# A fused attention and two-layer-MLP kernel: one weight loaded a step earlier, evictions placed ahead of conversion passes, and a lasting buffer for queries and keys

## The chip, the cores and the metric

The kernel runs on one core of a Trainium2 chip. The metric is the device time of one execution in microseconds (us); the number quoted for a kernel is the median of its runs. Before the change it is 1781.75 us (three runs, 1778.74 to 1783.21).

## The reference

Eight sequences of 576 tokens go through three stages. `q`, `k` and `v` have 8 heads of 64 columns; the model width is 512, the hidden width 2048.

```python
# 1: attention inside chunks of 64 tokens, head by head
scores = scale * np.matmul(q_c, k_c.transpose(0, 1, 2, 4, 3))
attn = softmax(scores)                      # last axis, max subtracted
x = heads_side_by_side(np.matmul(attn, v_c))
# 2: layer norm and a two-matmul block with its residual
xn = (x - mu) / np.sqrt(var + 1e-06) * g_ln
x = x + np.maximum(xn @ w_ch1, 0.0) @ w_ch2
# 3: a rank-32 mix over the tokens, then a second block
u = x + (x.transpose(0, 2, 1) @ U @ V).transpose(0, 2, 1)
out = u + np.maximum(u @ w2_ch1, 0.0) @ w2_ch2
```

The weights `U`, `V` and the four matrices arrive as 64-bit floats and are turned into 32-bit ones on the chip, by a handful of bit operations on each tile.

## The kernel before, in words

The 4608 tokens are 36 tiles of 128. Stage 1 and 2 work on 12 groups j = 0 to 11 of three tiles, stage 3 on 9 groups j = 12 to 20 of four. A group meets 16 slices f of the hidden width. One pair (j, f) is one **step** g of the main loop (lines 841 to 864): `g1` (line 638) issues twelve matmuls into the tile `psh`, then ScalarE writes the high part of the ReLU (line 648) and VectorE the low part (line 649); then the loop issues whatever `plan[g]` holds; then `g2` (line 650) multiplies the step two back into the accumulators `acc`, and after f = 15 `finish` (line 665) has VectorE add the accumulators to the residual (line 668), which frees their PSUM banks. Every product is made of three float32r matmuls (high by high, high by low, low by high). The first matmul of the next group into an accumulator waits for that eviction.

Groups 0 and 1 alternate in steps 2 to 31; from step 32 a group has 16 steps in a row. Steps 0 to 27 also convert the first set of weights; a PSUM bank for `psh` is single up to step 31 and doubled later.

All else is hung into the steps by `at(g, fn, ...)`, by hand (`manual_schedule`): each engine runs its instructions in the order in which the program issues them, and a DMA is issued by an engine too. SyncE issues the loads of `q`, `k`, `v` and the stores; ScalarE issues the second set of weights (`load_w`, line 113) and the round trips through DRAM that transpose a tile (`spread` and `gather`, lines 539 and 545). So a DMA that has to wait on ScalarE holds the ReLU behind it.

What the change touches:

- `load_ut` (line 201), in step 27: four SyncE loads of `U` into a raw tile, then its conversion (`conv_act` on ScalarE, `conv_bits` and `conv_hi` on VectorE, lines 81 to 105, and lines 211 and 212). The conversion's scratch takes the buffer `q6` or `k6` in turn.
- `load_qk` (line 253): queries and keys of group j, as 32-partition pieces in 128-byte runs. A group of 6 chunks that lies in one sequence is 32 DMAs, one that crosses two sequences 64 (`chunk_runs` yields two runs; groups 4, 7 and 10). Each group takes a new tile in the one buffer `q6` and the one buffer `k6`, so that its first DMA waits until the last tile of the group before has been read. Lines 740 to 743 cut the DMAs into parts, one for a step: 4 parts from the 12th step after g = 16(n-1) for n = 2, 4 from the 8th for n = 3, 9 from the 4th for n = 4, else 9 from the 3rd, where n + 1 is the group loaded.
- `st_A` (line 308): two VectorE transposes (lines 311 and 312) read one tile's share of the two buffers. The scores' matmuls into `psm` (`st_Bd`) need them, in the next step or the one after.
- `pre_a`, `pre_b` and `pre_c` (lines 165 to 182): conversion of the second set of weights, one weight tile every three and a half steps from step 58 on: `pre_a` two ScalarE and two VectorE passes, `pre_b` three VectorE passes, `pre_c` a store issued by ScalarE. They stand in `plan[g]`, so ahead of `g2` and `finish` of the same step.

Of the kernel before, what the change touches and what calls it, by code (L numbers as in the profile page):

```python
# [18 lines left out]
def fused_kernel(ctx, tc, q, k, v, g_ln, w1_a, w2_a, U, V, w1_b, w2_b, out):  # L19
    nc = tc.nc  # L20
# [86 lines left out]
    def raw_tile():  # L107
        return rawp.tile([P, DM, 2], I32, tag="raw", name="raw")
# [89 lines left out]
    def conv_f32(raw, rows, n, out):  # L198
        return conv_hi(conv_bits(conv_act(raw, rows, n)), out)

    def load_ut():
        Ui = U.bitcast(I32)
        raw = raw_tile()
        v = raw.rearrange("p (t r) w -> p t (r w)", r=RK)
        nc.sync.dma_start(out=v[:, 0:4], in_=Ui[0:512].rearrange("(t p) r -> p t r", p=P))
        nc.sync.dma_start(out=v[0:64, 4], in_=Ui[512:576])
        nc.sync.dma_start(out=v[64:128, 4], in_=Ui[0:64])
        nc.sync.dma_start(out=v[:, 5:9], in_=Ui[64:576].rearrange("(t p) r -> p t r", p=P))
        o = ut[:, 0:9].rearrange("p t r -> p (t r)")
        a, c = conv_f32(raw, P, 9 * RK, o)  # L210
        nc.vector.tensor_tensor(out=c, in0=c, in1=a, op=ALU.mult)
        nc.vector.tensor_tensor(out=o, in0=o, in1=c, op=ALU.add)

        nc.gpsimd.memset(ut[0:64, 9], 0.0)
        nc.gpsimd.tensor_copy(out=ut[64:128, 9], in_=ut[64:128, 4])
        nc.gpsimd.memset(ut[64:128, 4], 0.0)
# [36 lines left out]
    def load_qk(j, part, parts_):  # L253
        todo = []
        for nm in ("q6", "k6"):
            if part == 0:
                qk[nm, j] = qkp.tile([P, 4, 4 * TPB, 32], F32, tag=nm, name=nm)
        for off, n, b, s0 in chunk_runs(2 * TPB * j, 2 * TPB):
            for nm, src in (("q6", q), ("k6", k)):
                for g in range(4):  # L260
                    for pr in range(4):
                        todo.append((
                            qk[nm, j][32 * g:32 * g + 32, pr, 2 * off:2 * (off + n), :],
                            src[b, 2 * pr + g // 2, s0:s0 + n * CH, (g % 2) * 32:(g % 2) * 32 + 32].rearrange("(a j) i -> j a i", j=32),
                        ))
        for o, i_ in todo[part * len(todo) // parts_:(part + 1) * len(todo) // parts_]:
            nc.sync.dma_start(out=o, in_=i_)  # L267
# [40 lines left out]
    def st_A(i):  # L308
        j, t = divmod(i, TPB)
        qt = t1.tile([P, 4, P], F32, tag="qt", name="qt")  # L310
        nc.vector.transpose(out=qt.rearrange("p h (a j) -> p h a j", a=4), in_=qk["q6", j][:, :, 4 * t:4 * t + 4, :])
        nc.vector.transpose(out=pl["k"][:, 0].rearrange("p h (a j) -> p h a j", a=4), in_=qk["k6", j][:, :, 4 * t:4 * t + 4, :])
        state["qt", i] = qt

    qn = {}
# [362 lines left out]
    with tc.manual_schedule():  # L678
# [14 lines left out]
        for n in range(2, NB + NB2):  # L693
            g = NF * (n - 1)
            ends = []
            for t, i in enumerate(tiles_of(n)):
                s = g + (0, 4, 6, 8)[t]
                if n == 2:
                    s = (10, 15, 24)[t]
                    at(s - 6, load_qk_nat, i)  # L700
                    at(s, st_A_pe, i)
                    at(s + 1, st_B, i)
                    at(s + 2, st_C, i)
                    at(s + 3, st_D, i)
                    at(s + 3, load_v, i + 1)
                    if t == 0:
                        at(5, kv_tiles, i)
                        at(6, load_v, i)
                    ends += [(pos[0, NF - 1] - 1 + t, st_N, i), (pos[0, NF - 1] + t, st_E_pe, i)]
                elif n < NB:  # L710
                    s = g + {3: (2, 5, 8), 4: (-1, 2, 5)}.get(n, (-2, 1, 5))[t]
                    at(s - (1 if n < 5 or t == 0 else 2), st_A, i)
                    at(s, st_Bd, i)
                    at(s + 1, st_Cd, i)
                    at(s + 2, gather, 2 * NT + i)
                    at(s + 3, st_T, i)
                    at(s + 5, st_D, i)
                    if i + 1 < NT:
                        at(s + 5, load_v, i + 1)
                    s += 4 if n == 3 else 6  # L720
                    at(s + (n == 3), st_N, i)
                    at(s + 1, st_S, i)
                    at(s + 2, gather, i)
                    at(s + 3, st_E, i)
                else:
                    at(s + 1, u_load, i)
                    r = i % 9
                    if r in (0, 4):
                        b = 2 * (i // 9) + (r == 4)
                        at(s - 5, z_load, b, 0)  # L730
                        at(s - 4, z_sum, b)
                        at(s - 4, z_load, b, 1)
                        at(s - 2, z_rep, b)
                    at(s + 2, st_U, i)
                    at(s + 4, st_US, i)
                    at(s + 5, gather, NT + i)
                    at(s + 6, st_UE, i)
            for x in sorted(ends, key=lambda x: (x[0], x[1] is st_N)):
                at(*x)
            if 2 <= n < NB - 1:  # L740
                parts_ = 4 if n < 4 else 9
                for part in range(parts_):
                    at(g + {2: 12, 3: 8, 4: 4}.get(n, 3) + part, load_qk, n + 1, part, parts_)
        for n in range(NB + NB2):
            g = pos[n, NF - 1] + 1
            at(g + LAG + 2, store, n)
# [20 lines left out]
        EARLY = (2, 4, 6, 8)  # L767
        for p in range(len(EARLY), NP):
            at(max(p - 4, 2), weight, p)
        at(27, load_ut)  # L770
        at(NF * (NB - 2) + 9, load_V)
        at(NF * (NB - 2) + 13, make_vst)
        PRE_G = 58
# [67 lines left out]
        for g in range(len(seq) + LAG + 3):  # L841
            if g < pos[1, 0] + LAG:
                banks.update(h=("h0", "m0"), m=("m1", "h1", "z"))
            elif g < 10:
                banks.update(h=("h0", "m0"), m=())
            elif g <= pos[0, NF - 1] + LAG:
                banks.update(h=("h0",), m=("m0",))
            elif g == pos[0, NF - 1] + LAG + 1:
                banks.update(h=("h0",), m=("m0", "acc1", "acc2"))
            elif g < 2 * NF:  # L850
                banks.update(h=("h0", "acc0"), m=("m0", "acc1", "acc2"))
            elif g <= 2 * NF + 1:
                banks.update(h=("h0",), m=("m0",))
            else:
                banks.update(h=("h0", "h1"), m=("m0",) if pos[NB, 0] + LAG - 1 <= g <= pos[NB, NF - 1] + LAG else ("m0", "m1"))
            if g < len(seq):
                g1(*seq[g])
            for fn, a in plan.get(g, ()):
                fn(*a)
            if LAG <= g < len(seq) + LAG:  # L860
                j, f = seq[g - LAG]
                g2(j, f)
                if f == NF - 1:
                    finish(j)


_INS = ["q", "k", "v", "moe_g_ln", "moe_w_ch1", "moe_w_ch2", "moe2_U", "moe2_V", "moe2_w_ch1", "moe2_w_ch2"]
# [21 lines left out]
```

## Time and profile before

| what | value |
|---|---|
| median of the runs | 1781.75 us |
| the profiled execution's own time | 1782.99 us |
| its span, first to last instruction | 1781.0 us |
| TensorE busy | 1719.9 us, 97% |
| VectorE, ScalarE, GpSimd busy | 779.1, 372.3, 184.1 us |
| mean granted TensorE clock | 0.988 of full |

The page counts matmuls as PE and weight loads as PEld; `psh` is the output of `g1`, `acc` of `g2`, `psm` of the attention. A timeline row gives the start and length of an instruction (or of several alike, with their count), its engine and line, output and inputs, and in brackets the idle time of the engine just before it and what ended that. A row of waits gives who waited for what, the sum, the number of times and the longest. In a row of windows the busy time of each engine stands with its instruction count, then PEclk, the granted TensorE clock as a share of 2.4 GHz (0.50 is 1.2 GHz), then the DMA engines' share and GB/s. SPq and ACTq are the instruction queues of SyncE and ScalarE; all rows are from the one profiled execution, in us from its start.

### The profile page before, as it was taken

What the parts mean: (1) busy time and instruction counts of PE and PEld (TensorE: products, weight loads), DVE (VectorE), ACT (ScalarE), POOL (GpSimd) and SP (SyncE); (2) the same over time, 40 slices, a digit from 0 to 9 for tenths busy, and PEclk for the clock granted to TensorE, in tenths of its full rate; (3) what the DMA queues carried; (4) which work ended last, traced back from release to release, by engine and by line L of the source; (5) the groups of instructions that cost most, each with busy time, mean ns of one, the idle gap of its engine ahead of it and who ended that gap; (6) DMA issues with size and microseconds to landing.
All of it is one profiled execution on the core that took longest, in us unless ns stands there. A gap on an engine that the chain in (4) does not pass through costs nothing.

```text
span 1781.0 us, 25335 instructions
## 1 busy us (share of the span) xinstructions
PE 1719.9 (97%) x9960; PEld 1458.7 (82%) x9960; DVE 779.1 (44%) x1496; ACT 372.3 (21%) x666; POOL 184.1 (10%) x199
## 2 busy tenths in 40 slices
PE   6799898999999999999999999999999999999999
PEld 5678787888888888888888888888888888888887
DVE  6898744466656666565645312121212121212111
ACT  4333311122122222222223211111111111111110
POOL 1000001011010110101111010101010101000000
PEclk8899999999999999999999999999999999999999
DMA  7343324446465564655436312221212121212100
GB/s 169 95 129 108 80 76 98 107 123 161 108 150 138 129 148 105 166 130 135 120 107 200 96 47 72 53 72 48 71 47 72 48 74 45 66 30 60 30 24 24
DMA packets 293095, 167.48 MB, mean 94 GB/s; under 512 B 189424, under 2 KB 251888, under 8 KB 292976
## 3 DMA queue, kind: packets, MB, share of 16 engines
q1 hardware_dynamic: 212048, 93.48, 20.3%
q10 hardware_dynamic: 80928, 72.39, 15.1%
q8 instruction: 78, 1.28, 0.3%
q14 instruction: 41, 0.34, 0.1%
HBM read 112.82 MB, written 52.95 MB: 93 GB/s over the span
## 4 chain that ended last, share of the span: by engine, by line
PE 83%; DVE 8%; DMA 3%; issue 2%; SPq 2%; ACT 1%; POOL 1%; ACTq 0%; DVEq 0%; POOLq 0%
PE psh L60 40%; PE acc L60 39%; PE psm L60 2%; DMA raw<-in_moe_w_ch 1%; PE zps L60 1%; DVE act L649 1%; DVE cvt L95 1%; DVE cvt L103 1%; SPq L294 1%; ACT act L648 1%; DMA k<-in_k 1%; SPq L267 0%; DVE cvt L104 0%; DVE bs L468 0%; DVE cvt L94 0%
## 5 line engine op out<-in xcount | busy, mean ns | idle before, releaser
L60 PE MATMUL psh<-act,w0h 128*128 128x384 f32 (+1 forms) x2688 | 756.5, 362 | 18.4 <-DVE act L649 13.0
L60 PEld LDWEIGHTS psh<-act,w0h 128*128 128x128 f32 x2688 | 503.2, 190 | 84.8 <-DVE act L649 16.3
L60 PE MATMUL psh<-act,w0l 128*128 128x384 f32 (+1 forms) x1344 | 486.8, 362 | 1.0 <-DVE w0l L147 1.0
L649 DVE SCALAR_TENSOR_TENSOR hk<-psh,hq 128x512 fp32r<-128x512 f32 (+1 forms) x160 | 108.6, 679 | 629.3 <-ACT hq L648 629.3
L60 PE MATMUL acc<-w1h,act 128*128 128x512 f32 x1056 | 366.1, 401 | 4.8 <-DVE x L668 3.9
L60 PEld LDWEIGHTS psh<-act,w0l 128*128 128x128 f32 x1344 | 255.4, 190 | 23.8 <-DVE w0l L147 1.4
L60 PE MATMUL acc<-w1h,hq 128*128 128x512 f32 x624 | 243.0, 389 | 0.0
L60 PE MATMUL acc<-w1l,hq 128*128 128x512 f32 x624 | 243.0, 389 | 0.0
L60 PE MATMUL acc<-w1h,hk 128*128 128x512 f32 x624 | 242.9, 389 | 0.0
L60 PEld LDWEIGHTS acc<-w1h,act 128*128 128x128 f32 x1056 | 198.9, 188 | 51.6 <-ACT act L648 6.8
L648 ACT ACTIVATE hq<-psh 128x512 fp32r<-128x512 f32 (+1 forms) x160 | 94.0, 588 | 647.6 <-PE psh L60 647.6
L60 PE MATMUL acc<-w1l,act 128*128 128x512 f32 x528 | 209.1, 396 | 0.0
L649 DVE SCALAR_TENSOR_TENSOR act<-psh,act 128x384 fp32r<-128x384 f32 x176 | 97.7, 555 | 232.2 <-ACT act L648 231.8
L648 ACT ACTIVATE act<-psh 128x384 fp32r<-128x384 f32 x176 | 86.2, 490 | 440.0 <-PE psh L60 268.5
L555 POOL TENSOR_TENSOR act<-wT,act 128x512 fp32r<-128x512 f32 x63 | 81.2, 1289 | 898.5 <-ACT act L554 888.9
L60 PEld LDWEIGHTS acc<-w1h,hq 128*128 128x128 f32 x624 | 117.1, 188 | 25.6 <-ACT hq L648 1.7
L60 PEld LDWEIGHTS acc<-w1h,hk 128*128 128x128 f32 x624 | 117.1, 188 | 24.4
L60 PEld LDWEIGHTS acc<-w1l,hq 128*128 128x128 f32 x624 | 117.1, 188 | 24.1
L60 PEld LDWEIGHTS acc<-w1l,act 128*128 128x128 f32 x528 | 99.4, 188 | 16.0
L472 POOL TENSOR_SCALAR rs<-mv 128x1 f32<-128x1 f32 x36 | 8.9, 247 | 526.5 <-DVE mv L470 518.3
L554 ACT CAST act<-wT 128x512 fp32r<-128x512 f32 x63 | 39.2, 622 | 99.3 <-DVE wT L552 99.3
L552 DVE STREAM_TRANSPOSE wT<-w 128x512 f32<-128x512 f32 x63 | 44.3, 703 | 7.2 <-DMA wd<-v_pl 2.8
(106 smaller groups left out, 1039.7 us busy)
## 6 DMA issues: line engine op xcount, KB each, us to landing
w<-sp ACTq DMA_DIRECT2D x90, 256.0 KB, 2.7
x1d<-x SPq DMA_DIRECT2D x36, 256.0 KB, 2.6
x<-x1d SPq DMA_DIRECT2D x36, 256.0 KB, 3.4
sp<-x ACTq DMA_DIRECT2D x144, 64.0 KB, 1.8
out<-x SPq DMA_DIRECT2D x36, 256.0 KB, 2.2
v_pl<-in_v SPq DMA_DIRECT2D x132, 64.0 KB, 2.7
raw<-in_moe_w_ch SPq DMA_DIRECT2D x64, 128.0 KB, 2.8
raw<-in_moe_w_ch SPq DMA_DIRECT2D x16, 512.0 KB, 3.7
```

The costliest lines, as they stand in the source:

```text
L60: nc.tensor.matmul(o, lhsT=l, rhs=r, start=start, stop=stop)
L95: nc.vector.scalar_tensor_tensor(out=bi, in0=hw, scalar=-0x40000000, in1=bi, op0=ALU.bitwise_and, op1=ALU.bitwise_or)
L103: nc.vector.scalar_tensor_tensor(out=c, in0=d, scalar=2.0 ** -20, in1=c, op0=ALU.mult, op1=ALU.add)
L294: nc.sync.dma_start(out=pl["vbd"][pp, :, c, 64 * h2:64 * h2 + 64] if E0 <= i < PE_T else pl["v"][pp, i % 2 if i < E0 else 0, :, c, :], in_ ...
L472: nc.gpsimd.tensor_scalar(out=rs, in0=mv[:, 1:2], scalar1=1e-6, scalar2=None, op0=ALU.add)
L552: nc.vector.transpose(out=x.rearrange("p k (a j) -> p a k j", a=4), in_=w.rearrange("p a (k i) -> p a k i", k=KT))
L554: nc.scalar.copy(out=hi, in_=x)
L555: nc.gpsimd.tensor_tensor(out=lo, in0=x, in1=f32(hi), op=ALU.subtract)
L648: nc.scalar.activation(out=hi, in_=ps, func=AF.Relu)
L649: nc.vector.scalar_tensor_tensor(out=lo, in0=ps, scalar=0.0, in1=f32(hi), op0=ALU.max, op1=ALU.subtract)
```

## The change

`U` is loaded in step 27 and converted in step 28. Queries and keys get one tile each in `q6` and `k6` for the whole of stage 1, so a DMA of the next group waits only for the reads of the part that it overwrites. Their DMAs are cut anew: 4 parts from the 13th step for n = 2; else 6 parts for a group in one sequence and 8 (n = 3) or 10 for one that crosses two; from the 5th step for n = 3, from the 4th for one run, from the 0th for two. In the steps in which a group from j = 2 on ends, `pre_a`, `pre_b` and `pre_c` are issued after `finish` instead of before `g2`.

```diff
--- before.py
+++ after.py
@@ -198,14 +198,18 @@
     def conv_f32(raw, rows, n, out):
         return conv_hi(conv_bits(conv_act(raw, rows, n)), out)
 
-    def load_ut():
+    uraw = {}
+
+    def load_U():
         Ui = U.bitcast(I32)
-        raw = raw_tile()
+        raw = uraw[0] = raw_tile()
         v = raw.rearrange("p (t r) w -> p t (r w)", r=RK)
         nc.sync.dma_start(out=v[:, 0:4], in_=Ui[0:512].rearrange("(t p) r -> p t r", p=P))
         nc.sync.dma_start(out=v[0:64, 4], in_=Ui[512:576])
         nc.sync.dma_start(out=v[64:128, 4], in_=Ui[0:64])
         nc.sync.dma_start(out=v[:, 5:9], in_=Ui[64:576].rearrange("(t p) r -> p t r", p=P))
+    def make_ut():
+        raw = uraw.pop(0)
         o = ut[:, 0:9].rearrange("p t r -> p (t r)")
         a, c = conv_f32(raw, P, 9 * RK, o)
         nc.vector.tensor_tensor(out=c, in0=c, in1=a, op=ALU.mult)
@@ -253,14 +257,14 @@
     def load_qk(j, part, parts_):
         todo = []
         for nm in ("q6", "k6"):
-            if part == 0:
-                qk[nm, j] = qkp.tile([P, 4, 4 * TPB, 32], F32, tag=nm, name=nm)
+            if nm not in qk:
+                qk[nm] = qkp.tile([P, 4, 4 * TPB, 32], F32, tag=nm, name=nm)
         for off, n, b, s0 in chunk_runs(2 * TPB * j, 2 * TPB):
             for nm, src in (("q6", q), ("k6", k)):
                 for g in range(4):
                     for pr in range(4):
                         todo.append((
-                            qk[nm, j][32 * g:32 * g + 32, pr, 2 * off:2 * (off + n), :],
+                            qk[nm][32 * g:32 * g + 32, pr, 2 * off:2 * (off + n), :],
                             src[b, 2 * pr + g // 2, s0:s0 + n * CH, (g % 2) * 32:(g % 2) * 32 + 32].rearrange("(a j) i -> j a i", j=32),
                         ))
         for o, i_ in todo[part * len(todo) // parts_:(part + 1) * len(todo) // parts_]:
@@ -308,8 +312,8 @@
     def st_A(i):
         j, t = divmod(i, TPB)
         qt = t1.tile([P, 4, P], F32, tag="qt", name="qt")
-        nc.vector.transpose(out=qt.rearrange("p h (a j) -> p h a j", a=4), in_=qk["q6", j][:, :, 4 * t:4 * t + 4, :])
-        nc.vector.transpose(out=pl["k"][:, 0].rearrange("p h (a j) -> p h a j", a=4), in_=qk["k6", j][:, :, 4 * t:4 * t + 4, :])
+        nc.vector.transpose(out=qt.rearrange("p h (a j) -> p h a j", a=4), in_=qk["q6"][:, :, 4 * t:4 * t + 4, :])
+        nc.vector.transpose(out=pl["k"][:, 0].rearrange("p h (a j) -> p h a j", a=4), in_=qk["k6"][:, :, 4 * t:4 * t + 4, :])
         state["qt", i] = qt
 
     qn = {}
@@ -738,9 +742,10 @@
             for x in sorted(ends, key=lambda x: (x[0], x[1] is st_N)):
                 at(*x)
             if 2 <= n < NB - 1:
-                parts_ = 4 if n < 4 else 9
+                runs = len(list(chunk_runs(2 * TPB * (n + 1), 2 * TPB)))
+                parts_ = 4 if n < 3 else 6 if runs == 1 else 8 if n == 3 else 10
                 for part in range(parts_):
-                    at(g + {2: 12, 3: 8, 4: 4}.get(n, 3) + part, load_qk, n + 1, part, parts_)
+                    at(g + {2: 13, 3: 5}.get(n, 4 if runs == 1 else 0) + part, load_qk, n + 1, part, parts_)
         for n in range(NB + NB2):
             g = pos[n, NF - 1] + 1
             at(g + LAG + 2, store, n)
@@ -767,7 +772,8 @@
         EARLY = (2, 4, 6, 8)
         for p in range(len(EARLY), NP):
             at(max(p - 4, 2), weight, p)
-        at(27, load_ut)
+        at(27, load_U)
+        at(28, make_ut)
         at(NF * (NB - 2) + 9, load_V)
         at(NF * (NB - 2) + 13, make_vst)
         PRE_G = 58
@@ -855,13 +861,18 @@
                 banks.update(h=("h0", "h1"), m=("m0",) if pos[NB, 0] + LAG - 1 <= g <= pos[NB, NF - 1] + LAG else ("m0", "m1"))
             if g < len(seq):
                 g1(*seq[g])
+            j, f = seq[g - LAG] if LAG <= g < len(seq) + LAG else (0, 0)
+            late = (pre_a, pre_b, pre_c) if f == NF - 1 and j > 1 else ()
             for fn, a in plan.get(g, ()):
-                fn(*a)
+                if fn not in late:
+                    fn(*a)
             if LAG <= g < len(seq) + LAG:
-                j, f = seq[g - LAG]
                 g2(j, f)
                 if f == NF - 1:
                     finish(j)
+            for fn, a in plan.get(g, ()):
+                if fn in late:
+                    fn(*a)
 
 
 _INS = ["q", "k", "v", "moe_g_ln", "moe_w_ch1", "moe_w_ch2", "moe2_U", "moe2_V", "moe2_w_ch1", "moe2_w_ch2"]
```

## Rows read from the trace of the kernel before

**Rows 1.** The page: busy time of each engine.
```profile
PE 1719.9 (97%) x9960; PEld 1458.7 (82%) x9960; DVE 779.1 (44%) x1496; ACT 372.3 (21%) x666; POOL 184.1 (10%) x199
```

**Rows 2.** Windows: from step 25 to group 11, and the rest.
```profile
186.00:960.00 774.00, 751.38 (x5261) 651.66 (x5260) 442.30 (x897) 172.82 (x323) 101.10 (x120) 0.99 0.49 125
960.00:1781.00 821.00, 817.32 (x3619) 677.05 (x3617) 182.14 (x279) 123.62 (x209) 71.45 (x56) 1.00 0.20 58
```

**Rows 3.** Waits of TensorE from 186 to 960 us.
```profile
PE psm L60 <- DVE kt_pl L312: 8.0, 4, 2.5
PE psh L60 <- DVE act L649: 7.3, 3, 4.9
PE acc L60 <- DVE x L668: 3.9, 3, 1.5
...
PE psh L60 <- POOL act L555: 0.9, 1, 0.9
PE acc L60 <- ACT act L648: 0.9, 1, 0.9
PE psh L60 <- ACT act L554: 0.6, 1, 0.6
```

**Rows 4.** Windows: four stretches behind waits of TensorE.
```profile
207.76:214.59 6.83, 3.91 (x12) 3.91 (x13) 3.46 (x9) 1.40 (x3) 0.33 (x2) 0.50 0.28 46
293.10:296.51 3.41, 3.41 (x30) 2.97 (x32) 1.16 (x2) 0.49 (x1) 0.00 (x0) 0.50 0.81 195
313.58:316.99 3.41, 3.41 (x12) 3.22 (x11) 0.10 (x1) 0.49 (x1) 0.00 (x0) 0.50 0.35 79
457.00:461.00 4.00, 3.49 (x45) 3.05 (x46) 2.99 (x8) 1.25 (x2) 1.30 (x1) 1.00 0.01 4
```

**Rows 5.** Timeline, steps 27 to 29: U and what waits for it.
```profile
204.78 0.59 SPq L208 DMA_DIRECT2D raw<-in_moe_U  x1
...
207.24 0.47 ACT L86 ACTIVATE cvt<-raw 128x288 f32<-128x288 f32 x1 [8.40 <-DMA raw<-in_moe_U]
...
210.08 0.55 DVE L649 SCALAR_TENSOR_TENSOR act<-psh,act 128x384 fp32r<-128x384 f32 x1
...
210.68 1.01 PE L60 MATMUL psh<-act,w0h 128*128 128x384 f32 x2 [4.92 <-DVE act L649]
```

**Rows 6.** Timeline, steps 32 to 34; then the landing times of line 267's DMAs.
```profile
225.61 2.01 SPq L267 DMA_DIRECT2D k<-in_k  x4
...
234.57 0.67 DVE L312 STREAM_TRANSPOSE kt_pl<-k 128x512 f32<-128x512 f32 x1
...
235.87 0.61 PE L60 MATMUL psh<-act,w0h 128*128 128x384 f32 x2 [0.93 <-DVE x L668]
...
DMA to landing us min/median/max: 1.6/2.3/5.9
```

**Rows 7.** Timeline of VectorE, end of group 3 (step 65).
```profile
396.53 0.76 DVE L413 TENSOR_TENSOR e<-psm,mx 128x256 f32<-128x256 f32 x2
...
399.61 1.88 DVE L668 TENSOR_TENSOR x<-acc,x 128x512 f32<-128x512 f32 x3
```

**Rows 8.** Timelines at steps 77 and 109: waits for group 6 and group 8's keys.
```profile
456.65 0.71 DVE L312 STREAM_TRANSPOSE kt_pl<-k 128x512 f32<-128x512 f32 x1 [3.87 <-DMA k<-in_k]
...
457.51 0.69 PE L60 MATMUL psm<-kt_pl,qt 64*64 64x64 f32 x32 [2.34 <-DVE kt_pl L312]
...
607.85 0.69 PE L60 MATMUL psm<-kt_pl,qt 64*64 64x64 f32 x32 [2.39 <-DVE kt_pl L312]
```

**Rows 9.** ScalarE's timeline near step 45, and SyncE's waits over the whole span.
```profile
291.28 0.49 ACT L648 ACTIVATE act<-psh 128x384 fp32r<-128x384 f32 x1 [7.93 <-DMA sp<-xn]
...
SPq L267 <- DMA sp<-xn: 36.1, 17, 4.3
```

**Rows 10.** Timeline: two halves of one weight tile, interleaved word by word.
```profile
433.37 0.67 ACT L169 ACTIVATE raw<-raw 128x512 f32<-128x512 uint32 x1
...
433.50 0.43 DVE L170 TENSOR_SCALAR v_pl<-raw 128x512 int32<-128x512 int32 x1 [2.40 <-ACT raw L168]
```

## The prediction, made before the change was run

> **What bounds the kernel now.** I read the page first: TensorE is busy 97% of the span, no other engine half of it [rows 1]. So only time in which TensorE stands still or runs at the low clock can be won. The windows say where that is: from 960 us on it idles 3.7 us in 821, and these steps the change does not touch; from 186 to 960 us it idles 22.6 us in 774 at a mean clock of 0.99 [rows 2]. The change touches nothing before that either, so nearly all that it can win lies in those 774 us. The waits of TensorE there are few and large [rows 3]: four on the key transpose (8.0 us), three on the low part of the ReLU (7.3), evictions of accumulators (3.9, and 0.9 put down to ScalarE, which ends nearly with the eviction), and 1.5 on the normalized activations. To these comes the clock: granted 0.50 for 6.83 us with 3.91 of matmuls and twice for 3.41 us full of matmuls [rows 4]; each microsecond of matmuls at half clock loses half, so 2.0 and twice 1.7 us.
>
> **U, step 27 to 29.** ScalarE stood 8.40 us before its first conversion pass, until U had landed, with the ReLU of step 28 queued behind it; VectorE then did its seven passes ahead of that step's low part at 210.08, and TensorE started step 29 at 210.68, 4.92 us late and at half clock [rows 5]. After the change the load is issued in the same place, so U lands as before at about 207.2, but ScalarE and VectorE reach the ReLU of step 28 first. Its low part waits for nothing but the last weight's conversion and is done at about the end of the matmuls ahead (205.8): the 4.92 and the 2.0 go. The conversion, 2.9 us of VectorE (207.19 to 210.08), still runs then, ahead of the low part of step 29. That one comes at about 210.7, when step 29's matmuls have been through some 4.8 us, as long as such a step takes: what is late next costs 0 to 1 us here, I take 0.4. Gain 6.5.
>
> Part of it is given back. The loads of group 3's queries and keys wait for the conversion's scratch buffer, whose last reader ends when it did, at 210.2. They are moved a step back in the program but start at the same moment, and SyncE issues the 32 of them at about 0.5 us each up to 227.6 [rows 6]. Such a load lands a median 2.3 us from its issue [rows 6]; the last is issued about 227.1, so it lands at 229.4. The key transpose of the group's first tile ran at 234.57; with 6.5 us won it is wanted at 228.1 and so waits 1.3 us. Behind it on VectorE stands group 1's eviction, for whose bank TensorE already waited 0.93 us [rows 6], so all of the 1.3 is on the path. Net gain of this part **5.2** (5 to 6.5).
>
> **Evictions.** At the end of group 3, VectorE had finished the softmax's subtraction at 397.29, then stood waiting for ScalarE's conversion passes, did its own two, and began to evict at 399.61; one accumulator takes a third of 1.88 us [rows 7]. Put first, the eviction starts at 397.3 and its first bank is free at 397.9, before TensorE asks at 398.9 (its matmuls resume at 400.44 after 1.52 of idling). The conversion passes come about 2 us later, and behind them the low part of the ReLU, which has a step of room with two banks. Four of the seven group ends from step 65 to 161 have such passes in their step: those are the three waits of 3.9 and the one of 0.9 [rows 3]. Two more have only a store there, one nothing. I take all **4.8** (4 to 4.8).
>
> **Keys.** At step 77 the key transpose waited 3.87 us for its data and TensorE 2.34; at step 109 TensorE waited 2.39 [rows 8]. Both groups lie in one sequence; their last loads stood in the plan two steps before the read, and were issued later still, since SyncE's load issues stop until transfers that ScalarE issued have landed, though they need none of their data (36.1 us in 17 waits) [rows 9]. The new plan ends two steps, some 9 us, earlier, and ahead of the last tile's value load, which stands and waits on the same queue. That covers a wait of 3.87. The other single-run groups, 5, 9 and 11, show no wait of TensorE now. Gain **4.7** (3 to 4.7).
>
> **Group 4, steps 40 to 48.** Its 64 loads go 16 to a step now and 8 to a step after, three steps earlier. Here lie the rest of the 8.0 (2.48 at step 47, 0.79 earlier), 2.07 of the 7.3, the 1.5 on normalized activations, and the two low-clock stretches [rows 3, 4]: without the 0.79, 2.07 + 2.48 + 1.5 + 3.4 = 9.5 us. But what TensorE waits for is not the loads: ScalarE held a ReLU 7.93 us because the issue of a tile's round trip ahead of it waited for its layer norm [rows 9], and that order stays. Fewer loads in flight shorten the gathers by a microsecond or so in two or three links of that chain. Between 0 and 9.5 I take **2.5**, a shortened 2.07 and perhaps the clock loss behind it: the row of ScalarE's wait is nearer to the lower end.
>
> On the clock the rows are not simple: it fell behind 4.92 and 2.07 us of idling, not behind 2.34 (457 to 461 us, clock 1.00) [rows 4]. The Trainium skill ("TensorE: Matmul & The Clock Gate", Part 1) has the clock fall when the array was idle for long enough and come back after sustained work. If only long gaps counted, the 1.7 inside my 2.5 would not come back by trimming a 2.07, and the sum would be 1.7 smaller.
>
> **New costs.** The lasting buffers add no instruction of weight; the number of loads is the same (32 or 64). Denser loads hold the ScalarE issues behind them longer; in groups 5 to 11 they go from 3.6 to 5.3 a step, or 7.1 to 6.4. Lower bound nothing: groups 7 and 10 had 7.1 a step and TensorE waited for no load there. Upper bound the whole 9.5 of group 4 at 16 a step, for each. I take 0, nearest to the 7.1 rows.
>
> **Sum.** 5.2 + 4.8 + 4.7 + 2.5 = 17.2 off the profiled execution's own 1782.99 gives 1765.8. That execution lies 1.2 above the median of the runs, so I say **1765** against 1781.75; with group 4 between 0 and 9.5 and the other bounds, 1757 to 1770.
>
> **Rivals.**
> - *Half of it.* Waits move rather than go: the keys are still late by a microsecond because SyncE still stops at ScalarE's transfers, group 4 keeps all, step 29 waits the upper 1 us. 1781.75 - (4.5 + 4 + 2) = 1771. For it: the 36.1 us of stops [rows 9]; against it: the nine microseconds of new room. The Trainium skill ("DMA: Bandwidth & Descriptors", Issuing engines are not separate DMA queues) also speaks for it: transfers from different engines interleave on the same DMA engines. Chance 0.14.
> - *The parts are not told apart.* If a read of one tile had to wait for every earlier load into the lasting buffer, the third tile of groups 3, 6 and 9 would wait for the first loads of the next group, which the plan puts ahead of it: three waits of about 2.4 us, 1765 + 7 = 1772. Against it: VectorE read one half of a word-interleaved weight tile at 433.50 while ScalarE was writing the other from 433.37 to 434.04 [rows 10]. Chance 0.05.
> - *Slower.* ScalarE's round-trip issues wait for the denser loads ahead of them to land, its ReLUs come too late for two banks, and TensorE idles and loses its clock as it did in group 4: 9.5 us for each of groups 5 to 11. Two such groups already cancel the sure 14.7; three make 1781.75 - 14.7 + 28.5 = 1796. It decides where more than about 7 loads a step hold ScalarE for over a step. Against it: groups 7 and 10. Chance 0.04.
> - *Nothing measurable*, gains and new waits in balance: 0.03.
>
> **How the numbers follow.** The forecast has 0.74. About 0.3%, 5.3 us, is what a measurement of this kernel can tell from no change. Faster by more than that means under 1776.4: the forecast, the first two rivals, less a little for their tails, 0.90; within it 0.06; slower 0.04. The range 1756 to 1773 takes in group 4's full 9.5 below and the first two rivals above.
>
> **What would show it.** Right: no wait of ScalarE for U, clock 1.00 from 200 to 225 us, and a wait on group 1's eviction grown from 0.9 to about 2.2; the eviction ahead of lines 168 to 178 at steps 65, 97, 129 and 145 and no wait of `acc` there; no wait of line 312 on keys at steps 77 and 109. Wrong: a new long ScalarE wait before a ReLU in steps with loads, waits of line 312 at steps 39, 83 or 131, or low clock after 300 us in places where there was none.

## The result and the profile after

The changed kernel takes 1765.33 us in the median of four runs (1764.13 to 1766.33), the kernel before 1781.63 beside it (four runs). The ratio is 0.9911, interval 0.9896 to 0.9927: faster by 16.3 us, and the forecast was 1765. The profiled execution went from 1782.99 to 1765.73, 17.3 us less where 17.2 was worked out. That the sum hits so closely is luck: errors in its terms cancel, so the terms are read one by one.

The page of the changed kernel, busy time of each engine, against [rows 1]:

```profile
PE 1716.0 (97%) x9960; PEld 1455.5 (83%) x9960; DVE 778.4 (44%) x1496; ACT 371.8 (21%) x666; POOL 183.4 (10%) x199
```

The same work on every engine, the same counts. What changed is the idle time and the clock. The windows of the changed kernel, against [rows 2] and the first of [rows 4] (the windows start earlier, as the kernel runs ahead):

```profile
186.00:945.00 759.00, 749.93 (x5268) 650.89 (x5267) 441.80 (x897) 173.58 (x325) 101.56 (x120) 1.00 0.50 128
945.00:1763.90 818.90, 815.06 (x3607) 674.97 (x3605) 181.35 (x278) 122.09 (x207) 70.38 (x55) 1.00 0.20 57
...
204.88:214.42 9.54, 9.54 (x51) 8.37 (x51) 6.99 (x15) 4.17 (x8) 0.33 (x2) 1.00 0.32 57
298.98:305.81 6.83, 6.35 (x46) 5.39 (x46) 3.16 (x8) 1.54 (x3) 1.28 (x1) 0.50 0.15 41
```

Up to group 11 TensorE idles 9.1 us now where it idled 22.6; the second half is as it was. Steps 29 and 30 (204.88 to 214.42 us) run at clock 1.00 without a gap; the wait ahead of step 29 and that step held the first half-clock stretch. A half-clock stretch is left at 299 us. The waits of TensorE in the first of these windows, against [rows 3]:

```profile
PE psm L60 <- DVE kt_pl L316: 5.0, 4, 3.0
PE psh L60 <- DVE act L653: 1.9, 2, 1.6
PE psh L60 <- DVE x L672: 1.1, 1, 1.1
PE acc L60 <- ACT e L421: 0.7, 1, 0.7
PE psh L60 <- POOL act L559: 0.2, 1, 0.2
```

(Line numbers of the changed kernel are four higher: 316, 653, 672, 271 for 312, 649, 668, 267.) The four waits of `acc` on the eviction at the group ends of [rows 3] are gone, and the 4.92 of step 29. Key transposes still cost 5.0: 3.0 and 0.8 in the stretch of steps 40 to 48 (at steps 47 and 40), 1.0 for the transpose of step 77. The 0.7 put down to line 421, at step 82, is new.

To place the gain I cut each trace into steps: a step starts with its first matmul into `psh`, twelve to a step. (A transpose that hangs in step 77 or 109 is waited for by matmuls of step 78 or 110, so the delay shows there.) Lengths in us, worked out from the profiled execution of each kernel (the experiments' edits stand below; bold where one differs from before by over 1):

| steps | 27-30 | 36-48 | 65-80 | 81-96 | 97-112 | 113-144 | 145-191 |
|---|---|---|---|---|---|---|---|
| before | 25.79 | 71.37 | 77.04 | 73.85 | 76.49 | 147.89 | 213.43 |
| after | **19.41** | **69.23** | **73.95** | 74.81 | **72.89** | **146.74** | **212.08** |
| e1_u | **19.35** | **69.96** | **78.53** | 73.85 | 75.72 | 147.89 | 213.23 |
| e2_evict | 25.53 | 71.51 | 76.98 | 73.85 | 76.25 | **146.74** | **211.45** |
| e3_loads | 25.89 | **68.86** | **74.66** | **74.91** | **74.02** | 147.89 | 213.22 |
| e4_buffer | 25.52 | **69.97** | **78.40** | 73.85 | 76.18 | 147.89 | 214.07 |

Steps 192 to 334 take 785.94 in both kernels. Step by step, the changed kernel wins 6.4 at steps 27 to 30 and gives 0.2 back by step 35; wins 2.1 at steps 36 to 48; 1.75, 1.15, 1.15 and 1.74 at the four evictions (steps 66, 98, 130 and 146); 1.37 and 2.43 at the keys, in steps 78 and 110; and loses 0.96 at step 82 and some 0.6 in small pieces. One more microsecond came before step 27, in code that the change does not touch. Together 17.3.

### The profile page after: what moved, and what is told of

Its sections match the earlier page's. It is cut to its first block, busy times and chain, and to the rows that moved or that the text cites. A ratio compares the mean times of both kernels' runs of the same rounds, so it can differ in the third digit from the quotient of the medians.

```text
span 1763.9 us, 25347 instructions
## 1 busy us (share of the span) xinstructions
PE 1716.0 (97%) x9960; PEld 1455.5 (83%) x9960; DVE 778.4 (44%) x1496; ACT 371.8 (21%) x666; POOL 183.4 (10%) x199
## 4 chain that ended last, share of the span: by engine, by line
PE 84%; DVE 7%; DMA 3%; issue 2%; SPq 2%; ACT 1%; POOL 1%; ACTq 0%; DVEq 0%; POOLq 0%
PE psh L60 40%; PE acc L60 40%; PE psm L60 3%; SPq L271 1%; PE zps L60 1%; DVE cvt L95 1%; DVE act L653 1%; DMA raw<-in_moe_w_ch 1%; DVE cvt L103 1%; DMA k<-in_k 1%; DVE cvt L94 0%; ACT act L652 0%; DMA sp<-xn 0%; DVE w0l L147 0%; DVE cvt L104 0%
## 5 line engine op out<-in xcount | busy, mean ns | idle before, releaser
L672 DVE TENSOR_TENSOR x<-acc,x 128x512 f32<-128x512 f32 x72 | 45.0, 680 | 4.8 <-PE acc L60 4.8
```

The lines of the kernel that those rows point to most:

```text
L672: nc.vector.tensor_tensor(out=x, in0=acc.pop((j, t)), in1=x, op=ALU.add)
```

## The experiments: the parts alone

My theory was the sum of the prediction: four independent parts. The main rival was that a wait removed in one place comes back in another, so that the parts alone would win less or more than in company. Four kernels start from the one before, each with one part.

**U alone**

```diff
-    def load_ut():
+    def load_U():
...
+    def make_ut():
...
-        at(27, load_ut)
+        at(27, load_U)
+        at(28, make_ut)
-   at(g + {2: 12, 3: 8, 4: 4}.get(n, 3) + part, load_qk, ...)
+   at(g + {2: 13, 3: 8, 4: 4}.get(n, 3) + part, load_qk, ...)
```

> The kernel before with one part of the change alone: U loaded in step 27, converted in step 28 (and group 3's loads therefore one step later). Theory (each part returns the waits that it removes, and they add): the 4.92 us wait and the 1.95 us of half clock go, 0.2 to 0.4 is given back, so 6.2 us off, about 1775.4. Rival (the loads behind the conversion become what is late): the key transpose of step 33 waits over a microsecond for them and 5 us or less are left, about 1776.7. The trace decides at the wait of line 668's eviction: near 1.1 us by the first, over 2 by the second.

Measured: 1774.46 against 1780.67, ratio 0.9962 (0.9948 to 0.9976), 6.2 us. Steps 27 to 30 take 19.35, as in the whole change. The waits of TensorE (186 to 945 us):

```profile
PE psm L60 <- DVE kt_pl L316: 7.9, 4, 3.1
PE acc L60 <- DVE x L672: 3.9, 3, 1.5
PE psh L60 <- DVE act L653: 2.4, 2, 2.2
PE psh L60 <- DVE x L672: 1.2, 1, 1.2
PE acc L60 <- ACT act L652: 0.9, 1, 0.9
```

The evictions stand as before, and the key transposes in sum, 7.9 where they cost 8.0 [rows 3]; single key waits moved by up to 0.7 us. The wait on group 1's eviction is 1.2, near the 1.1 expected. Steps 65 to 80 are 1.49 longer than before: half clock behind the key wait (last section).

**Evictions alone**

```diff
+            j, f = seq[g - LAG] if LAG <= g < len(seq) + LAG else (0, 0)
+            late = (pre_a, pre_b, pre_c) if f == NF - 1 and j > 1 else ()
             for fn, a in plan.get(g, ()):
-                fn(*a)
+                if fn not in late:
+                    fn(*a)
...
-                j, f = seq[g - LAG]
                 g2(j, f)
                 if f == NF - 1:
                     finish(j)
+            for fn, a in plan.get(g, ()):
+                if fn in late:
+                    fn(*a)
```

> The kernel before with the eviction alone put ahead of the conversion passes in the step that ends a group. Theory: the four waits of the accumulators at steps 65, 97, 129 and 145 go and nothing takes their place, 4.8 to 5.8 us off, about 1776. Rival (VectorE is simply full there, and a delayed pass holds the next ReLU instead): new waits of psh on line 649 one or two steps later, and under 2 us off, 1780.

Measured: 1777.41 against 1780.67, ratio 0.9976 (0.9967 to 0.9986), 3.3 us. The waits on `acc` are gone, the rest stands:

```profile
PE psm L60 <- DVE kt_pl L312: 7.4, 4, 2.5
PE psh L60 <- DVE act L649: 7.3, 3, 4.9
PE psh L60 <- DVE x L668: 0.9, 1, 0.9
```

The step lengths say 5.8 for the four evictions, the medians 3.3 (by the interval 2.5 to 5.9), under the 4.8 to 5.8 expected. In the profiled execution the difference lies in two rows of the table: at steps 65 to 80 1.75 was won and 0.06 is left, at 97 to 112 1.15 and 0.24, because the key waits there were followed by half clock, which they were not in the profile of before (last section). Whether that held in the other executions no trace shows.

**Key and query loads alone** (lasting buffer and the new plan)

```diff
-            if part == 0:
-                qk[nm, j] = qkp.tile(..., tag=nm, name=nm)
+            if nm not in qk:
+                qk[nm] = qkp.tile(..., tag=nm, name=nm)
...
-                parts_ = 4 if n < 4 else 9
-                    at(g + {2: 12, 3: 8, 4: 4}.get(n, 3) + part, load_qk, ...)
+                parts_ = 4 if n < 3 else 6 if runs == 1 else 8 if n == 3 else 10
+                    at(g + {2: 12, 3: 5}.get(n, 4 if runs == 1 else 0) + part, load_qk, ...)
```

> The kernel before with the lasting query and key buffers and the denser, earlier loads alone (group 3's loads where they were). Theory: the step-109 wait for keys goes (2.4), the one of step 77 shrinks to about 1.0 (1.4), group 4's stretch gives back about 2, and about 1 is lost at the end of group 4 (step 82), where the loads of group 7 now start: 4 to 5 us off, about 1777. Rival (the gain of the whole change is U and the evictions): 1 us or less off, 1781.

Measured: 1775.44 against 1780.67, ratio 0.9971 (0.9961 to 0.9981), 5.2 us.

```profile
PE psh L60 <- DVE act L649: 7.3, 3, 5.1
PE acc L60 <- DVE x L668: 3.9, 3, 1.5
PE psm L60 <- DVE kt_pl L312: 3.5, 3, 1.9
...
PE acc L60 <- ACT e L417: 0.8, 1, 0.8
```

No key wait is left at step 77 or 109, though about 1.0 was expected to stay at step 77. With the same load plan the whole change does wait 1.00 there, and three more profiles of it without the loads put first (group 3's order, group 7 late, the changed kernel again) wait 0.7 to 1.0. In the loads alone four key loads were left behind ScalarE's transfer and the last landed 5.4 us after step 77 began; in the whole change five were left and it took 6.4. Step 66, which the eviction still makes 1.75 longer here, gave SyncE that much more time. So part of what the evictions win is paid back at the keys; that this is the reason is read from these times and was not tried by itself. Of the three waits left two lie in the stretch of steps 40 to 48 (at 269.51 and 307.08). One of 0.79 at 378.52 is new, and no load is behind it: that transpose follows the low part of a ReLU on VectorE without idling, and the low part had waited 1.76 us for ScalarE. The new 0.8 on the attention's exponential, the 0.7 of the whole change, comes with this part: steps 81 to 96 take 74.91 here and 73.85 in the kernels with the old plan.

**The lasting buffer alone**, with the old plan:

```diff
-            if part == 0:
-                qk[nm, j] = qkp.tile(..., tag=nm, name=nm)
+            if nm not in qk:
+                qk[nm] = qkp.tile(..., tag=nm, name=nm)
...
```

> The kernel before with the lasting buffers alone, every load in its old step. Theory (the old plan never asked a load to run ahead of the last read, so the buffer only permits the new plan): no change, 1781.6 within 1.5 us, and the waits of 2.3 to 2.4 us for keys at steps 77 and 109 stay. Rival (the loads were held by the release of the whole buffer): those waits shrink, 3 us or more off.

Measured: 1781.91 against 1780.67, ratio 1.0005 (0.9994 to 1.0017): no change. The key waits stay (8.5 us in five). The buffer wins nothing by itself; it lets a group's loads start before the last tile of the group ahead has been read, which the old plan never asked for.

The three parts win 6.2 + 3.3 + 5.2 = 14.7 us by their medians, the whole 16.3 and, measured once more below, 15.0. Within the intervals (each part is known to some 2 us) the parts add up, and the rival of waits that only move falls but for the 1 us of keys at step 77.

## The experiments: what stayed or came new

Three places are taken up, where waits were left or new: steps 45 to 47 (1.57 and 3.01, and half clock behind them), step 77 (1.00), step 82 (0.73). Four kernels start from the changed one.

**Group 4 without its loads.** This kernel leaves out the loads of group 4's queries and keys; the rest is as in the changed kernel.

```diff
     def load_qk(j, part, parts_):
+        if j == 4:
+            return
```

> The changed kernel without the 64 loads of group 4's queries and keys (steps 37 to 44): its scores are made from what the buffers still hold, so group 4's attention is left out of the comparison and only the time is read. Theory (TensorE's stalls of 1.57 us at step 45 and 3.01 us at step 47, and the half clock behind them, come from ScalarE standing at the issue of a tile's round trip until its layer norm is done, not from the loads): both stalls stay within half a microsecond to a microsecond of their size, the time falls by 0 to 2 us. Rival (loads in flight delay the chain): both go, 6 to 8 us off, about 1758.

Measured: 1762.69 against 1780.65, ratio 0.9899 (0.9884 to 0.9914), 2.6 us less than the changed kernel. Waits of TensorE from 278 to 322 us:

```profile
PE psm L60 <- DVE kt_pl L318: 2.3, 1, 2.3
PE psh L60 <- DVE act L655: 1.3, 1, 1.3
```

With no load in flight for group 4, both stalls stand, 1.3 and 2.3 where they were 1.6 and 3.0. But steps 36 to 48 take 66.87, where five profiles with the new plan's loads have 68.6 to 69.5, and the time fell by a little more than the 2 us expected. So the loads cost this stretch some 2 us, half of it in these waits and much of the rest in the clock (half clock for 3.41 us instead of 6.83); they do not make the stalls.

**Group 3, its tiles a step earlier.** Tiles 1 and 2 do everything up to the layer norm a step earlier, while the round trip's issue (`st_S`, line 542) stays in its step:

```diff
-   s = g + {3: (2, 5, 8), 4: (-1, 2, 5)}.get(n, (-2, 1, 5))[t]
+   s = g + {3: (2, 4, 7), 4: (-1, 2, 5)}.get(n, (-2, 1, 5))[t]
...
-   at(s + 1, st_S, i)
-   at(s + 2, gather, i)
-   at(s + 3, st_E, i)
+   d = n == 3 and t > 0
+   at(s + d + 1, st_S, i)
+   at(s + d + 2, gather, i)
+   at(s + d + 3, st_E, i)
```

> The changed kernel with group 3's second and third tile begun one step earlier, and for these two the round trip issued one step after the layer norm instead of in its step. Theory (ScalarE's queue stood at that issue): the waits of 1.57 and 3.01 us at steps 45 and 47 shrink to under 1 us in sum and the clock stays at 1.00 there: 5 to 8 us off, about 1758. Rival (the chain from value product to next group's first matmul is too long by itself): the stall comes back at step 48, on the last normalized activations, 0 to 2 us off.

Measured: 1761.00 against 1780.65, ratio 0.9888 (0.9874 to 0.9902), 4.3 us less than the changed kernel's 1765.33. Steps 36 to 48 take 63.56 where they took 69.23. ScalarE's timeline of the changed kernel at steps 44 to 47:

```profile
281.04 2.07 ACTq L546 DMA_DIRECT2D sp<-xn  x4
...
283.64 0.49 ACT L652 ACTIVATE act<-psh 128x384 fp32r<-128x384 f32 x1 [7.74 <-DMA sp<-xn]
...
294.83 2.08 ACTq L546 DMA_DIRECT2D sp<-xn  x4
297.02 0.49 ACT L652 ACTIVATE act<-psh 128x384 fp32r<-128x384 f32 x1 [7.33 <-DMA sp<-xn]
```

and of this kernel at the same steps:

```profile
278.55 1.78 ACTq L546 DMA_DIRECT2D sp<-xn  x4
280.43 0.49 ACT L652 ACTIVATE act<-psh 128x384 fp32r<-128x384 f32 x1 [5.29 <-DMA sp<-xn]
...
291.02 2.19 ACTq L546 DMA_DIRECT2D sp<-xn  x4
293.32 0.49 ACT L652 ACTIVATE act<-psh 128x384 fp32r<-128x384 f32 x1 [4.74 <-DMA sp<-xn]
```

The four issues of a round trip stand ahead of a ReLU on ScalarE, and wait for the layer norm. With the layer norm a step ahead of them, ScalarE's ReLU stands 2.5 us less, and the windows (the changed kernel, then this one) show both stalls and the half clock gone together:

```profile
278.00:322.00 44.00, 39.42 (x267) 33.50 (x266) 18.76 (x41) 6.82 (x13) 6.74 (x8) 0.92 0.30 68
```

```profile
278.00:322.00 44.00, 42.58 (x296) 36.12 (x294) 18.53 (x41) 6.93 (x13) 5.16 (x6) 1.00 0.29 65
```

What idling is left there, 1.4 us, waits for normalized activations at step 48, the place that the rival named, and a wait of 0.9 is new at step 39; so the medians win 4.3, a little under the 5 to 8 expected. This is the cause that [rows 9] named and that the change left in place. The edit moves the attention ahead of the layer norm along with it, so what it shows is that these tiles' chain, up to the issue, was a step too late.

**Group 5 to 11's loads ahead in their step**, and one group's later by a step: a part of loads is put first in its step's plan, ahead of ScalarE's `st_S` and the other work of the step; group 5's start a step later.

```diff
-   at(g + {2: 13, 3: 5}.get(n, 4 if runs == 1 else 0) + part, load_qk, n + 1, part, parts_)
+   s = g + {2: 13, 3: 5, 4: 5}.get(n, 4 if runs == 1 else 0) + part
+   plan.setdefault(s, []).insert(0 if n > 3 else len(plan.get(s, ())), (load_qk, (n + 1, part, parts_)))
```

> The changed kernel with each part of the loads of groups 5 to 11 put at the front of its step, ahead of ScalarE's transfers of that step (group 5 starts one step later for that). Theory (SyncE's load issues stop until ScalarE's transfers that stand ahead of them in the program have landed): the last loads go out earlier and the wait of 1.00 us for keys at step 77 goes; ScalarE's transfers then stand behind loads instead, which may cost a step its ReLU: between 2 us off and 1 us more. Rival (the loads wait for the DMA engines, not for that order): the 1.00 us stays and nothing changes, 1765 within 1 us.

Measured: 1763.67 against 1780.65, ratio 0.9904 (0.9890 to 0.9918): within the intervals the changed kernel's time, so the verdict is read from the wait in question. The timeline of the changed kernel at step 77, SyncE's and ScalarE's issues and who waits:

```profile
436.19 1.79 ACTq L546 DMA_DIRECT2D sp<-xn  x4
...
437.86 2.37 SPq L271 DMA_DIRECT2D k<-in_k  x5
...
444.53 0.71 DVE L316 STREAM_TRANSPOSE kt_pl<-k 128x512 f32<-128x512 f32 x1 [2.53 <-DMA w<-sp]
445.39 0.69 PE L60 MATMUL psm<-kt_pl,qt 64*64 64x64 f32 x32 [1.00 <-DVE kt_pl L316]
```

The last five key loads are issued only when the four transfers of ScalarE's spread, issued from 436.19 on, land: the first load at 437.86, 0.02 us after the first of them has landed. The transpose stands 2.53 us (the last key lands at 444.35), TensorE 1.00. With the loads put ahead of the spread, the last is issued before 436.7 (SyncE's and VectorE's timelines of this kernel, which runs 4 us ahead by then):

```profile
425.86 10.81 SPq L271 DMA_DIRECT2D k<-in_k  x11
436.90 1.33 SPq L298 DMA_DIRECT2D v_pl<-in_v  x2
...
440.20 0.71 DVE L316 STREAM_TRANSPOSE kt_pl<-k 128x512 f32<-128x512 f32 x1 [0.73 <-DMA k<-in_k]
```

TensorE has no key wait at step 77 here, and steps 65 to 80 take 73.33 instead of 73.95. SyncE's waits over the whole span say that the change left the stops themselves as they were, 37.9 us in 19 against 36.1 in 17 [rows 9], and in this kernel they are 38.0 in 19; only the place of one has moved. The row of the changed kernel:

```profile
SPq L271 <- DMA sp<-xn: 37.9, 19, 6.1
```

**Group 7 on the old plan**, 9 parts from the third step instead of 10 from the 0th:

```diff
-   parts_ = 4 if n < 3 else 6 if runs == 1 else 8 if n == 3 else 10
-   at(g + {2: 13, 3: 5}.get(n, 4 if runs == 1 else 0) + part, load_qk, ...)
+   parts_ = 4 if n < 3 else 6 if runs == 1 else 8 if n == 3 else 9 if n == 6 else 10
+   at(g + {2: 13, 3: 5, 6: 3}.get(n, 4 if runs == 1 else 0) + part, load_qk, ...)
```

> The changed kernel with group 7's loads where they were before (9 parts from the 3rd step instead of 10 from the 0th). Theory (the new wait of 0.73 us at step 82 comes from ScalarE's weight-load issues standing behind these loads): it goes, 1 us off, 1764, which is at the edge of what can be told; the trace decides by that wait. Rival (it comes from the eviction's place): it stays.

Measured: 1763.15 against 1780.65, ratio 0.9899 (0.9885 to 0.9913). The profile has steps 81 to 96 at 73.85, the length of before, and no wait at step 82, which decides; 2.2 us of median are at the edge of what can be told. ScalarE's timeline there and VectorE's eviction of group 4, the changed kernel, then this one:

```profile
455.20 5.25 ACTq L120 DMA_DIRECT2D raw<-in_moe_w_ch  x4
460.49 0.49 ACT L652 ACTIVATE act<-psh 128x384 fp32r<-128x384 f32 x1 [5.32 <-PE acc L60]
463.74 1.88 DVE L672 TENSOR_TENSOR x<-acc,x 128x512 f32<-128x512 f32 x3
```

```profile
455.18 1.89 ACTq L120 DMA_DIRECT2D raw<-in_moe_w_ch  x4
458.83 0.49 ACT L652 ACTIVATE act<-psh 128x384 fp32r<-128x384 f32 x1 [3.70 <-DMA raw<-in_moe_w_ch]
462.08 1.88 DVE L672 TENSOR_TENSOR x<-acc,x 128x512 f32<-128x512 f32 x3
```

ScalarE's four weight loads took 5.25 us to issue beside SyncE's loads of group 7, 1.89 without them. The ReLU behind them came 1.7 us later (460.49 against 458.83), behind it on VectorE the low part, the softmax's passes and the eviction of group 4, each as much later (463.74 against 462.08). The first matmul into `acc` started at 464.57, when a third of the 1.88 us of eviction, one bank, was done (464.4). So the 0.73 is a wait for an eviction again, although the profile puts it down to line 421, which ended at nearly the same time (464.49). Long issues beside loads were not enough for it: in the kernel before, four weight loads at step 137 took 4.63 us beside ten key and query loads, and TensorE waited for nothing there; at step 81 a group ends. That is the new cost of the change, of the kind of the rival "Slower" (here weight loads hold the ReLU, not round trips, and the clock stays up), at a tenth of its price.

## The experiments: a version with what they showed

The last three edits together, and the changed kernel once more on the same chip, unchanged.

```diff
+   s = g + {3: (2, 4, 7), 4: (-1, 2, 5)}.get(n, (-2, 1, 5))[t]
+   d = n == 3 and t > 0
...
+   parts_ = 4 if n < 3 else 6 if runs == 1 else 8 if n == 3 else 9 if n == 6 else 10
+   s = g + {2: 13, 3: 5, 4: 5, 6: 3}.get(n, 4 if runs == 1 else 0) + part
+   plan.setdefault(s, []).insert(0 if n > 3 else len(plan.get(s, ())), (load_qk, (n + 1, part, parts_)))
```

> The three edits that helped (loads at the front of their step, group 3's earlier tiles, group 7's loads as late as before) together in the changed kernel. Theory (they remove different waits, so they add): from the changed kernel 1.0 at step 77, 1.0 at step 82 and 4 to 6 in steps 36 to 49 go: 6 to 8 us off the changed kernel, about 1758, and TensorE idles under 4 us from step 36 to 176. Rival (loads at the front hold ScalarE's round trips in group 3's new order): no better than the 1761 of group 3's order alone.

> The changed kernel as it is, on the same chip and beside the same runs of the kernel before as the combination. All theories: 15 to 17 us under the kernel before; its stretch from step 36 to 49 again between 68.5 and 70 us, with two waits at steps 45 and 47, if these belong to the program and not to one execution.

Measured: 1758.25 (ratio 0.9876, 0.9859 to 0.9892) and 1765.12 (0.9911, 0.9896 to 0.9926), both against 1780.14: 6.9 us less than the changed kernel, the fastest of all. Window of the combined kernel:

```profile
186.00:945.00 759.00, 754.48 (x5302) 655.35 (x5301) 444.39 (x901) 176.45 (x330) 103.12 (x122) 1.00 0.51 129
```

TensorE idles 4.5 us there, where the changed kernel idled 9.1 and the one before 22.6 in a window of nearly that length; from step 36 to 176 it idles 3.0, under the 4 expected. The changed kernel's second profile has steps 36 to 48 at 69.53 and the two waits again (1.6 and 3.4 us at steps 45 and 47).

## Why the prediction was right, term by term

- **U: 5.2 forecast, 6.2 came.** The load landed and the conversion ran when forecast, and what was called late next, the low part of step 29, cost nothing:

```profile
203.80 0.59 SPq L210 DMA_DIRECT2D raw<-in_moe_U  x1
204.28 0.55 DVE L653 SCALAR_TENSOR_TENSOR act<-psh,act 128x384 fp32r<-128x384 f32 x1
...
206.22 0.31 DVE L94 TENSOR_SCALAR cvt<-raw 128x288 int32<-128x288 int32 x1 [0.73 <-DMA raw<-in_moe_U]
...
209.11 0.55 DVE L653 SCALAR_TENSOR_TENSOR act<-psh,act 128x384 fp32r<-128x384 f32 x1
```

  The first ReLU row stands ahead of the conversion now, the second right behind its end. The step that failed is the 1.3 given back on group 3's keys. I let SyncE need 17.4 us for the 32 loads, as in the trace of before; it needed 16.4 (209.22 to 225.59), so the last key landed at 227.30, just as VectorE came to them (227.38), and the wait on group 1's eviction grew from 0.93 to 1.15, not to 2.2.
- **Evictions: 4.8 forecast, 5.8 came** in the step lengths. The order is the one forecast (VectorE's timeline, end of group 3, against [rows 7]):

```profile
387.50 0.76 DVE L417 TENSOR_TENSOR e<-psm,mx 128x256 f32<-128x256 f32 x2
388.17 1.88 DVE L672 TENSOR_TENSOR x<-acc,x 128x512 f32<-128x512 f32 x3
389.97 0.42 DVE L170 TENSOR_SCALAR v_pl<-raw 128x512 int32<-128x512 int32 x1
```

  Each of the four steps got shorter by about 0.24 more than its wait row says, so a row of waits slightly understates what such a wait costs the step.
- **Keys: 4.7 forecast, 3.8 came.** The failed step is "that covers a wait of 3.87", worked out for this part by itself. Two steps of room did cover step 109, and the loads alone covered step 77 too; with the evictions' gain in front of it the last loads of step 77 still stood behind ScalarE's spread, and 1.00 stayed. That is the first condition of the rival "Half of it", right for one of two places; its other two conditions did not come. The Trainium skill ("DMA: Bandwidth & Descriptors", Issuing engines are not separate DMA queues) says that transfers started by different engines run on the same DMA engines and interleave. The trace agrees: of the five loads beside the spread and a weight load, four landed 4.5 to 4.9 us after their issue, where the median is 2.3 [rows 6]. But the runs show more than that: an issue on one engine was itself held until another engine's transfer had landed.
- **Group 4: 2.5 forecast, 2.1 came**, and not safely: kernels with the old plan took 70.0 to 71.5 us for steps 36 to 48, those with the new plan's loads 68.6 to 69.5 (five executions). The means of the two are 1.7 us apart. The gathers shortened by less than the microsecond or so that I gave them: the third to fifth of this stretch landed in the mean 3.7 us after their issue with the old plan (four profiles) and 3.4 with the new one (five); without any loads they took 2.6 to 2.8. And the gain is not where I put it. The failed step is "a shortened 2.07 and perhaps the clock loss behind it": the 2.07 lost 0.5 and the 2.48 behind it gained as much, the clock loss went from 3.4 to 3.2, and it is the 1.5 on normalized activations that nearly all went (0.2 left). The reading that ScalarE's queue, more than the loads, sets this stretch is borne out by the two experiments on it: 66.87 without the loads, 63.56 with the layer norm earlier. The far end of 9.5 was out of this change's reach; another edit, the layer norm a step earlier, took 5.7 more from this stretch in its profile.
- **New costs: 0 forecast, 1.0 came** at step 82. The failed step is the choice of the nearest row: groups 7 and 10 had 7.1 loads a step without a wait, and I took 6.4 a step to be harmless. But the rate was not what mattered. Group 7's loads were moved beside the four weight loads that ScalarE issues just ahead of the end of group 4, and the ReLU held there holds an eviction. One of the signs of "wrong" came with it, a longer ScalarE wait before a ReLU (5.32 us where it was 3.70).
- **Start: 1.0 less** before step 27, untouched code, a chance of the two executions: in the twelve profiles step 27 starts anywhere from 193.1 to 198.1 us.

Errors of +1.0, +1.0, -0.9, -0.4 and -1.0, small losses of 0.6 and the chance microsecond make the sum hit to 0.1; that is luck. What was right is the mechanism of the first two terms and, but for step 77, of the third: the waits named went, by the way named. The rival of false waits on the lasting buffer is out: no key wait at steps 39, 83 or 131, and the buffer alone at 1.0005.

## What to carry to other kernels

Look at what stands behind a waiting instruction on its own engine, and move either of the two by one step: U (6.2 us), the evictions (5.8 by the steps, 3.3 by the medians) and the layer norm of group 3 (4.3 by the medians) were the same fault, work that waits placed ahead of work that does not. When loads are made denser or earlier, look not at their number a step but at which issues of the other engine stand beside them and at what waits behind those. Putting loads with a due time ahead of the other engine's transfers in the same step took the key wait away, though the time alone does not tell it from no change. A gain in one place can bring forward what was just in time in another, as at step 77. A lasting buffer is worth only what the plan does with it.

## What the runs showed of the hardware

Waits of like length cost unlike amounts. In the profile of before, 2.34 us of idling at step 77 left the clock at 1.00 [rows 4, 8]. In the kernels with the old plan for the keys, 2.41 us (U alone), 2.48 (evictions alone) and 2.13 (buffer alone) at the same step put it to 0.50; the windows of the evictions alone behind its two key waits:

```profile
454.48:457.89 3.41, 3.41 (x9) 2.65 (x9) 1.58 (x6) 1.25 (x2) 1.28 (x1) 0.50 0.02 5
604.67:608.08 3.41, 3.41 (x10) 2.64 (x9) 2.04 (x7) 2.34 (x4) 1.28 (x1) 0.50 0.00 0
```

Two stretches of 3.41 us full of matmuls at half clock lose 1.7 us each; the second came behind a gap of only 1.75 us. In the profile of the buffer alone, 2.08 us at step 110 left it at 1.00. So such a wait costs about its length, or 1.7 more, and one profile does not tell which. In the profiled execution of the evictions alone that accounts for the gap between the 5.8 of the four steps and the 3.3 of the medians. The Trainium skill ("TensorE: Matmul & The Clock Gate", Part 1) has the clock fall when the array was idle for long enough; gaps of 3.01 and 4.92 us agree. Between 1.7 and 2.5 us the length alone did not decide here: the clock fell behind 1.75 and stayed up behind 2.39.

ScalarE's and SyncE's DMA issues hold one another in both directions: key loads stood until a spread had landed (step 77), and weight-load issues took 5.25 us instead of 1.89 beside SyncE's loads (step 82). The traces show what an issue waits for, though it needs none of the other's data. The 1399 DMAs of the two engines use eight completion semaphores between them. Of the 384 key and query loads from 209 us on in the changed kernel, 361 wait for one semaphore alone, the one that they themselves will use. So such a load goes out when the last DMA on that semaphore has landed, whichever engine issued it: at 437.86 behind a transfer of the spread that landed at 437.84; and ScalarE's weight loads at 457.10 and 460.06 behind SyncE's loads that landed at 457.08 and 460.04. That is the program's assignment of semaphores. Whether other assignments would take the stops away was not tried.
